# Attention, gated MLP and top-1 mixture of experts on one core: wider weight conversions, paired reciprocals, gate dots over eight steps, an earlier gather, and unscaled q with a mask per head

## The chip, the cores and the metric

One of the eight cores of a Trainium2 chip runs the whole program in one launch. The metric is device microseconds per execution. Three executions of the kernel before took 839.56, 837.05 and 837.06 us; the median is 837.06 us, and lower is better.

## What is computed

```python
# attention: 4 batches, 8 heads, 576 positions, 64 per head
scores = q @ k.T / 8 - slope[h] * abs(rel), where 0 <= rel < 128, else -1e9   # slope[h] = 2 ** -(h + 1)
x = softmax(scores) @ v                        # 2304 tokens, 512 wide
# gated MLP, 512 -> 1536 -> 512
x = ((x @ w_a) * (x @ w_b)) @ w_out
# top-1 mixture of 8 experts
logits = x @ w_gate + modality_bias[modality_id]
out = prob_of_best * (relu(x @ w1[best]) @ w2[best])
```

Inputs and output are float32. `w_a`, `w_b` and `w_out` come as float64 and are cut to float32 on the chip by integer operations on their two 32-bit words.

## The kernel before, in words

**Work.** The 2304 tokens are 18 tiles of 128, in seven chunks `c` of 3, 2, 2, 3, 3, 3 and 2 tiles. For a chunk, attention is done one (head pair `hp`, tile `t`) item at a time, 12 items for chunk 0, and then the MLP runs over 12 steps `j` of 128 hidden columns: 24 matmuls for the two products (L512), a product of the two on VectorE, and the output matmuls (L525 in chunk 0, L529 after it), which are issued one step late. While chunk `c` is in its MLP, the items of chunk `c+1` are woven in. The last part gathers tokens by expert: a first big tile of 384 tokens, then five more (`big(u)`, u = 0 to 4), a small one of 64 tokens that starts inside u = 2, and what is left under conditions.

**Float32 products.** Most matmuls run in the type float32r, with each operand split into a high and a low part and three products taken. A split is a copy on ScalarE (the high part) and a subtraction on VectorE (the low part).

**Order.** All of attention of chunk 0 is ordered by hand (`manual_schedule`, L756 to L850): every engine takes its instructions in program order there. Each turn `g` of the loop at L802 holds, for several items at once, the transposes of item g (`pt_tr`), the products with v of item g-1 (`pv_mm`), the transposed output of item g-2 (`pv_tr`), the scores of item g+3 (`score_mm`), then on VectorE `score_sel` and `score_max` (L255, L261), `score_inv` (L275, L276: add 1e-9, reciprocal), and on ScalarE the copy of the transposed weights (`pt_cp`, L303; the two triangles are then cut out on GpSimd, L311 and L313), two exponentials (`score_exp`, L271) and the scaling of the output by the reciprocals (`pv_ev`, L341 on VectorE for the first head of the pair and L344 on ScalarE for the second). `conv_step` puts one or two weight conversion operations into a turn, from g = CVS = 1 on. Outside the parts ordered by hand a planner orders each engine's instructions by priority (program order, with some lines raised) and by when it takes them to be ready.

**q of chunk 0.** The scores of a head pair are taken with one array `qq` that has each head's 64 rows of q and zeros in the other 64, so that one load of k serves both. `a_load` loads q into `raw` (L156), k (L157) and v (L158); `a_prep_q` writes q, times a scale that holds 1/8 and the inverse of the head's slope, into `qq`: seven ScalarE operations (L207) and one VectorE operation (L204). With that scale one mask serves all heads: `score_max` adds `base` or `first` and multiplies by minus the slope. `make_masks` (L95 to L113) builds the masks on GpSimd and VectorE, and `qq_zero` (L184) clears the other halves on GpSimd.

**Conversions.** For each step `j` the two weights are six VectorE operations on 128x512 words (L429, L433, L437, three for each weight) and for each weight a copy on ScalarE (L444) and a subtraction on VectorE (L445). The float32 results sit in the tag `x2`, of three buffers. `slot0` (L975) does step `j+2`'s in step `j` of chunk 0, and three more operations for `w_out`.

**Gate.** For a tile of chunk 0 to 5, the eight logits are eight products with a row of `w_gate` broadcast over the partitions and summed on VectorE (`rd_dot`, L596). `rd_fetch` loads two rows (512 KB, tag `wo`, four buffers shared with `w_out`'s); steps 0 to 3 of the next chunk each fetch two rows and take both products for all tiles, then `rd_fin` does the routing.

**Gather.** `big(u)` reads the expert's number and the offset into registers of SyncE, loads the indices (L915, SyncE's queue), gathers the rows (L918, three indirect DMAs on GpSimd's queue), and loads W1 and W2 (L895, L906, SyncE's queue). At u = 2 the small tile's index, rows and weights are queued behind these. The gathered rows are transposed on TensorE (L934) while the tile before is still in its second product.

## Time and profile before

| | |
|---|---|
| three runs | 839.56, 837.05, 837.06 us; median 837.06 |
| the profiled execution's own time | 840.08 us |
| its span, first to last instruction | 838.4 us |
| granted TensorE clock, mean over the span | 0.994 |
| busy in the span: TensorE, VectorE, ScalarE, GpSimd | 812.3, 557.2, 429.8, 182.1 us |
| bytes moved | 145.37 MB, 173 GB/s in the mean |

All durations below are from the profiled execution. Times in a window or a timeline are microseconds from the span's start. Matmuls are pipelined and their ends are modelled, so a busy TensorE can still be one that is held up; what holds it is read from the waits and the chain. PE is TensorE, DVE VectorE, ACT ScalarE, POOL GpSimd, SPq SyncE's DMA queue; L12 is line 12.

### The profile page before, as it was taken

The numbers are of one execution on the slowest core, as the hardware profiler recorded it, in microseconds if no ns is written. First come the engines' busy times: TensorE is split into PE (matmuls) and PEld (weight loads), VectorE is DVE, ScalarE is ACT, GpSimd is POOL, SyncE is SP. The second block draws the span as 40 slices with busy tenths as digits, with TensorE's granted clock in tenths as the row PEclk, the third lists the DMA queues.
The fourth block names the chain that finished last, engine by engine and source line by source line (L and its number), as shares of the span: only waits on it lengthen the run. The fifth ranks groups of instructions, "written<-read, shape, count | busy, mean of one in ns | idle before, by whom it ended". The sixth has DMA issues, their size and how long they took to land.

```text
span 838.4 us, 14297 instructions
## 1 busy us (share of the span) xinstructions
PE 812.3 (97%) x4770; PEld 730.6 (87%) x4770; DVE 557.2 (66%) x1699; ACT 429.8 (51%) x1144; POOL 182.1 (22%) x245
## 2 busy tenths in 40 slices
PE   8899999999999989999999999999999999999994
PEld 6788877989989979999999999999988998979893
DVE  7799996987976875568865693377376444447320
ACT  6754465647666735665556632232336444537420
POOL 5322012113222222212222111100133030115101
PEclk9999999999999999999999999999999999999998
DMA  9995445786674774444642253647328553538301
GB/s 260 339 401 188 137 140 169 206 284 200 190 213 149 186 211 131 117 120 139 180 130 89 76 186 105 200 163 223 134 82 303 193 185 123 185 117 294 123 27 40
DMA packets 67874, 145.37 MB, mean 173 GB/s; under 512 B 12047, under 2 KB 32175, under 8 KB 67792
## 3 DMA queue, kind: packets, MB, share of 16 engines
q1 hardware_dynamic: 64240, 134.64, 51.6%
q0 software_dynamic: 3552, 9.73, 3.2%
q8 instruction: 40, 0.66, 0.3%
q14 instruction: 42, 0.34, 0.1%
HBM read 122.35 MB, written 22.12 MB: 172 GB/s over the span
## 4 chain that ended last, share of the span: by engine, by line
PE 75%; issue 8%; DMA 5%; DVE 5%; ACT 3%; POOL 2%; SPq 1%; POOLq 0%; ACTq 0%; DVEq 0%
PE ps_ab L512 32%; PE acc L529 13%; PE ps_h L1129 8%; PE ps_y L1112 7%; PE ps_o L369 4%; PE acc L525 4%; PE ps_s L247 2%; DMA wgt<-in_wgt 2%; PE ps_p L297 1%; PE ps_o L334 1%; PE ps_t L934 1%; PE ps_s L243 1%; DVE junk L596 1%; ACT p L271 1%; POOL out L1119 1%
## 5 line engine op out<-in xcount | busy, mean ns | idle before, releaser
L512 PE MATMUL ps_ab<-xr,wab 128*128 128x384 f32 (+1 forms) x2016 | 345.1, 318 | 4.7 <-DVE gf L1071 3.2
L512 PEld LDWEIGHTS ps_ab<-xr,wab 128*128 128x128 f32 x2016 | 308.5, 188 | 16.9 <-DVE gf L1071 4.7
L529 PE MATMUL acc<-wo,g 128*128 128x512 f32 x540 | 143.9, 398 | 0.0
L311 POOL TENSOR_SCALAR_AFFINE_SELECT pt<-pc 128x512 fp32r<-128x512 f32 (+1 forms) x72 | 50.4, 700 | 330.1 <-DVE pc L309 189.6
L529 PEld LDWEIGHTS acc<-wo,g 128*128 128x128 f32 x540 | 96.5, 188 | 15.3
L1129 PE MATMUL ps_h<-xT,w1s 128*128 128x384 f32 x576 | 104.2, 337 | 0.0
L1112 PE MATMUL ps_y<-w2s,h 128*128 128x512 f32 x432 | 104.1, 394 | 0.0
L1129 PEld LDWEIGHTS ps_h<-xT,w1s 128*128 128x128 f32 x576 | 99.7, 188 | 1.4 <-issue 0.5
L596 DVE CUSTOM_DVE_ANT_0 junk<-x,wgt 128x512 f32<-128x512 f32 x128 | 91.8, 717 | 12.2 <-DMA wgt<-in_wgt 8.0
L1112 PEld LDWEIGHTS ps_y<-w2s,h 128*128 128x128 f32 x432 | 79.8, 188 | 15.8
L271 ACT ACTIVATE p<-p,mx 128x128 f32<-128x128 f32 x144 | 56.8, 396 | 31.3 <-DVE mx L261 30.7
L1074 ACT CAST g<-gf 128x256 fp32r<-128x256 f32 (+1 forms) x72 | 33.0, 458 | 58.2 <-DVE gf L1071 57.9
L1071 DVE TENSOR_TENSOR gf<-ps_ab,asb 128x256 f32<-128x256 f32 (+1 forms) x72 | 35.1, 487 | 38.1 <-PE ps_ab L512 34.3
L1067 ACT COPY asb<-ps_ab 128x256 f32<-128x256 f32 (+1 forms) x72 | 30.6, 424 | 58.2 <-PE ps_ab L512 57.4
L885 DVE TENSOR_TENSOR w2s<-wr,w2s 128x1024 fp32r<-128x1024 f32 x24 | 29.4, 1225 | 38.4 <-ACT w2s L884 38.1
L313 POOL TENSOR_SCALAR_AFFINE_SELECT pt<-pc 128x512 fp32r<-128x512 f32 (+1 forms) x72 | 54.7, 760 | 0.0
L885 DVE TENSOR_TENSOR w1s<-wr,w1s 128x1024 fp32r<-128x1024 f32 x28 | 34.3, 1224 | 23.9 <-ACT w1s L884 23.9
L284 ACT ACTIVATE p<-p,mx 128x128 f32<-128x128 f32 x104 | 36.0, 394 | 25.3 <-DVE mx L276 23.8
L369 PE MATMUL ps_o<-pt,vv 128*128 128x256 f32 x312 | 48.8, 290 | 0.0
L1119 POOL DMA_INDIRECT out<-y,idx x18 | 21.4, 1187 | 116.0 <-ACT y L1118 114.5
L255 DVE COPY_PREDICATED ps_s<-upper,ps_s 128x256 f32<-128x256 uint8 x72 | 30.5, 424 | 23.8 <-PE ps_s L247 16.5
L1132 ACT ACTIVATE h<-ps_h 128x384 fp32r<-128x384 f32 x48 | 23.4, 489 | 43.7 <-PE ps_h L1129 43.7
(218 smaller groups left out, 1136.0 us busy)
## 6 DMA issues: line engine op xcount, KB each, us to landing
wo<-wo_d SPq DMA_DIRECT2D x60, 512.0 KB, 3.8
wr<-in_moe_w SPq DMA_DIRECT2D x56, 512.0 KB, 4.3
wgt<-in_wgt SPq DMA_DIRECT2D x24, 512.0 KB, 4.3
wraw<-in_moe_w_a SPq DMA_DIRECT2D x12, 512.0 KB, 8.4
wraw<-in_moe_w_b SPq DMA_DIRECT2D x12, 512.0 KB, 9.1
wor<-in_moe_w_out SPq DMA_DIRECT2D x12, 512.0 KB, 4.4
kr<-in_k SPq DMA_DIRECT2D x24, 256.0 KB, 4.2
wo_d<-wo SPq DMA_DIRECT2D x12, 512.0 KB, 3.3
```

The lines of the kernel that those rows point to most:

```text
L271: nc.scalar.activation(out=it.p[:, h, :], in_=it.p[:, h, :], func=AF.Exp, bias=it.mx[:, 2 + h:3 + h], scale=-1.0, accum_out=it.mx[:, 4 + h ...
L284: nc.scalar.activation(out=it.p[:, h, :], in_=it.p[:, h, :], func=AF.Copy, scale=it.mx[:, 6 + h:7 + h])
L311: nc.gpsimd.affine_select(out=it.pt[:, :, 0], in_=pc, pattern=pat + [[-1, P]], base=0, channel_multiplier=1, compare_op=ALU.is_gt, fill=0.0)
L313: nc.gpsimd.affine_select(out=it.pt[:, :, 1], in_=pc, pattern=pat + [[1, P]], base=0, channel_multiplier=-1, compare_op=ALU.is_ge, fill=0.0)
L369: nc.tensor.matmul(it.po, lhsT=a.vv[:, t + b, r].rearrange("p h d -> p (h d)"), rhs=it.pt[:, :, b, s, :], start=(i == 0), stop=(i == 5))
L512: nc.tensor.matmul(ps[:, :n], lhsT=w[:, m, r, kk * P:(kk + 1) * P], rhs=xr[:, s, kk, :n], start=(idx == 0), stop=(idx == len(terms) - 1))
L529: nc.tensor.matmul(acc[c, t], lhsT=g[:, r, t * P:(t + 1) * P], rhs=w[:, s, :], start=(j == 0 and idx == 0), stop=(j == NJ - 1 and idx == 2))
L596: nc.vector.tensor_tensor_reduce(out=junk, in0=x2[:, 0:DM], in1=wgt[:, k], scale=1.0, scalar=0.0, op0=ALU.mult, op1=ALU.add, accum_out=lgr ...
L885: nc.vector.tensor_tensor(out=dst[:, 1], in0=srcw, in1=dst[:, 0], op=ALU.subtract)
L1071: nc.vector.tensor_tensor(out=gf[:, :n], in0=psb[:, :n], in1=asb[:, :n], op=ALU.mult)
L1112: nc.tensor.matmul(pss[t], lhsT=h[:, r, f, t * P:(t + 1) * P], rhs=W2[f // 2][:, s_, f % 2, :], start=(f == 0 and i == 0), stop=(f == 7 an ...
L1129: nc.tensor.matmul(ps, lhsT=W1[f // 2][:, r, kk, (f % 2) * P:(f % 2 + 1) * P], rhs=xT[:, s_, kk, :], start=(kk == 0 and i == 0), stop=(kk ...
```

## The change

1. **Paired conversions.** `wab_jobs` does both weights of a step in one operation of 1024 words each: three VectorE operations, one ScalarE copy and one subtraction, in place of six, two and two. The float32 result has a tag of its own, `ff`, with one buffer. In chunk 0's attention they begin at g = 3 in place of 1, always one at a time, and stop when four are left.
2. **Paired reciprocals.** In chunks 0 and 1 two items share a tile for their sums, and the addition and the reciprocal are done once for both, at the second.
3. **Dots over eight steps.** Each of steps 0 to 7 takes one row's products; the load of two rows is in every other step.
4. **Gather ahead.** `big(u)` emits the index load and the gathers of `u+1` after its tenth group of matmuls, where it was at the start of `big(u+1)`.
5. **q unscaled.** Chunk 0's q is loaded straight into the two halves of `qq`, by two DMAs of 64 partitions in place of one of 128; `a_prep_q` does nothing there. Each head has its own pair of masks, `fb` (first and base) times 2^(2-h): two made on VectorE, six on GpSimd, ahead of the clearing of the later pairs' halves. The scale in `score_max` is -1/8 there.
6. In `pv_ev`, the first head's scaling goes to ScalarE for chunk 0's first six items. The SBUF set aside for GpSimd's DMA descriptors is 8192 bytes of a partition.

```diff
-    CVS = 1
+    CVS = 3
@@ make_masks
+        for h in range(H):
+            if h % 4 == 0:
+                mh = m1.tile([P, 4, 2, P], BF16, tag="x2", bufs=3, name="m_h")
+            masks[h] = mh[:, h % 4]
+            (nc.vector if h < 2 else nc.gpsimd).tensor_scalar(out=masks[h], in0=fb, scalar1=2.0 ** (2 - h), scalar2=None,
+                                                              op0=ALU.mult)
@@ a_load, c == 0
-            nc.sync.dma_start(out=a.qr, in_=q[rows, 0:q1])
+            for h in range(2):
+                o = 64 * h
+                nc.sync.dma_start(out=a.qq[o:o + 64, h, 0:q1], in_=q[hp * P + o:hp * P + o + 64, 0:q1])
@@ a_prep_q
+        if a.c == 0:
+            return
@@ score_max
+            if a.c == 0:
+                m, sc = masks[2 * a.hp + h][:, min(it.t, 1)], -0.125
@@ score_inv
+        if it.a.c in V32:
+            if it.half:
+                m = it.mxp
+                nc.vector.tensor_scalar(out=m[:, :, 4:6], in0=m[:, :, 4:6], scalar1=1e-9, scalar2=None, op0=ALU.add)
+                nc.vector.reciprocal(out=m[:, :, 6:8], in_=m[:, :, 4:6])
+            return
@@ pv_ev
-            if it.a.c == 0 and h == 0:
+            if it.a.c == 0 and h == 0 and it.a.hp >= 2:
@@ wab_jobs
+        def one():
+            f = m1.tile([P, 2, KD * P], U32, tag="ff", bufs=1, name="f64f")
...
+        def sp():
+            f = st[0].bitcast(F32)
+            w = wab[j] = wab_p.tile([P, 2, 2, KD * P], F32R, tag=f"wab{j}", name=f"wab{j}")
+            nc.scalar.copy(out=w[:, :, 0], in_=f)
+            nc.vector.tensor_tensor(out=w[:, :, 1], in0=f, in1=w[:, :, 0], op=ALU.subtract)
+
+        return [("d", one), ("d", lambda: more(1, 0xC0000000, ALU.bitwise_and)),
+                ("d", lambda: more(0, 29, ALU.logical_shift_right)), ("s", sp)]
@@ rd_dot
-        for k in range(2):
-            for i, t, x2, lgr in rd:
...
+        for i, t, x2, lgr in rd:
+            junk = m1.tile([P, DM], F32, tag="x2T", bufs=1, name="junk")
+            nc.vector.tensor_tensor_reduce(out=junk, in0=x2[:, 0:DM], in1=wgt[:, e % 2], scale=1.0, scalar=0.0,
+                                           op0=ALU.mult, op1=ALU.add, accum_out=lgr[:, e:e + 1])
@@ conv_step
-            if g >= CVS and len(conv) > 8:
-                kd = conv[0][0]
-                for _ in range(2 if kd == "s" else 1):
-                    if conv and conv[0][0] == kd:
-                        conv.pop(0)[1]()
+            if g >= CVS and len(conv) > 4:
+                conv.pop(0)[1]()
@@ main loop
-            if rd and R0 <= j < R0 + E // 2:
-                wgt = rd_fetch(2 * (j - R0))
+            if rd and R0 <= j < R0 + E and (j - R0) % 2 == 0:
+                wgt = rd_fetch(j - R0)
@@ big
-        pool = side()
-        idx, xg = u_gather(ld(uv, NBIG + u, E * RG - UT), 3, pool)
+        if u not in pre:
+            pre_gather(u)
+        pool, idx, xg = pre.pop(u)
...
+            if ahead and n_ == S_P:
+                pre_gather(u + 1)
@@ kernel
-    nc = bacc.Bacc("TRN2", target_bir_lowering=False, num_devices=1)
+    nc = bacc.Bacc("TRN2", target_bir_lowering=False, num_devices=1, dynamic_dma_scratch_size=8192)
```

## Rows read from the trace of the kernel before

**Rows 1.** The page, part 1: busy time and share of the span, TensorE.
```profile
PE 812.3 (97%) x4770; PEld 730.6 (87%) x4770; DVE 557.2 (66%) x1699; ACT 429.8 (51%) x1144; POOL 182.1 (22%) x245
```

**Rows 2.** Waits of TensorE over the span: total us, times, longest us.
```profile
PE ps_ab L512 <- DVE gf L1071: 3.2, 3, 2.0
PE ps_t L934 <- DMA xg<-x2d,idx: 1.6, 1, 1.6
```

**Rows 3.** Windows between the first score matmuls of successive items, chunk 0.
```profile
11.01:13.10 2.09, 2.09 (x18) 1.94 (x17) 1.61 (x8) 1.52 (x9) 0.88 (x3) 1.00 1.05 375
13.10:16.33 3.23, 2.42 (x17) 1.94 (x16) 2.86 (x11) 2.17 (x8) 0.51 (x2) 1.00 1.20 217
16.33:20.18 3.85, 3.58 (x15) 2.64 (x16) 3.58 (x19) 3.42 (x13) 2.65 (x7) 0.80 0.89 289
20.18:23.15 2.97, 2.97 (x16) 2.50 (x16) 1.44 (x9) 1.17 (x6) 1.55 (x4) 0.68 1.02 388
...
28.52:31.57 3.05, 2.25 (x18) 1.97 (x17) 2.19 (x7) 2.01 (x8) 0.51 (x2) 1.00 1.00 318
31.57:34.53 2.96, 2.53 (x16) 1.91 (x16) 2.93 (x15) 2.90 (x11) 2.15 (x6) 1.00 1.01 401
sum 26.42, PE 23.50 PEld 18.33 DVE 21.02 ACT 19.90 POOL 10.71; mean PE 2.61 PEld 2.04 DVE 2.34 ACT 2.21 POOL 1.19
```

**Rows 4.** Groups by line and shape, window 0 to 43.3.
```profile
L207 ACT ACTIVATE kk<-raw,qscale 64x384 f32<-64x384 f32 x7 | 4.3, 612 | 1.1 <-DMA raw<-in_q 1.0
L344 ACT ACTIVATE u<-ps_o,mx 128x64 f32<-128x64 f32 x12 | 3.7, 310 | 6.0 <-DVE u L341 5.9
```

**Rows 5.** Timeline, first 18 us: start, duration, instruction, [idle before].
```profile
1.26 0.42 SPq L157 DMA_DIRECT2D kk<-in_k  x1
4.03 2.91 PEld L243 LDWEIGHTS ps_s<-kk 128*128 128x128 f32 x12 [0.59 <-POOL kk L184]
7.08 0.11 POOL L724 MEMSET osum<- 128x8 bf16 x1
9.12 0.41 POOL L311 TENSOR_SCALAR_AFFINE_SELECT pt<-pc 128x256 f32<-128x256 f32 x1 [1.93 <-ACT pc L303]
17.28 0.67 DVE L437 SCALAR_TENSOR_TENSOR f64f<-wraw,f64f 128x512 uint32<-128x512 uint32 x1
17.37 0.84 POOL L311 TENSOR_SCALAR_AFFINE_SELECT pt<-pc 128x256 f32<-128x256 f32 x1 [3.77 <-ACT pc L303]
```

**Rows 6.** The page, part 6: DMA issues, KB each, us to landing.
```profile
wo<-wo_d SPq DMA_DIRECT2D x60, 512.0 KB, 3.8
kr<-in_k SPq DMA_DIRECT2D x24, 256.0 KB, 4.2
```

**Rows 7.** Groups by line and shape, window 50 to 130.
```profile
L433 DVE SCALAR_TENSOR_TENSOR f64f<-wraw,f64f 128x512 uint32<-128x512 uint32 x19 | 12.8, 689 | 0.0
L444 ACT CAST wab<-f64f 128x512 fp32r<-128x512 f32 x20 | 11.4, 617 | 5.9 <-DVE f64f L437 5.8
```

**Rows 8.** Lines L445 and L525: duration ns min/median/max, first and last start us.
```profile
L445 DVE TENSOR_TENSOR wab<-f64f,wab x24: 665/682/884, 29.5 to 128.0; 128x512 fp32r<-128x512 f32 x24
L525 PE MATMUL acc<-f64f,gf x72: 591/592/648, 51.8 to 144.9; 128*128 128x512 f32 x72
```

**Rows 9.** Windows of chunks 1 to 3: PE, PEld, DVE, ACT, POOL busy, clock, DMA.
```profile
150.00:180.00 30.00, 28.66 (x204) 26.21 (x203) 29.65 (x83) 17.77 (x51) 4.82 (x6) 1.00 0.78 240
...
212.00:245.00 33.00, 31.64 (x236) 29.68 (x235) 32.32 (x117) 22.45 (x75) 10.58 (x12) 1.00 0.72 219
...
280.00:306.00 26.00, 23.21 (x139) 21.43 (x138) 18.07 (x62) 14.24 (x44) 4.63 (x7) 1.00 0.87 216
```

**Rows 10.** Timeline of VectorE, chunk 3: start, duration, instruction, [idle before].
```profile
301.70 0.69 DVE L596 CUSTOM_DVE_ANT_0 junk<-x,wgt 128x512 f32<-128x512 f32 x1 [5.96 <-DMA wgt<-in_wgt]
```

**Rows 11.** Timeline of SyncE's queue in tile u = 2.
```profile
719.55 10.86 SPq L906 DMA_DIRECT2D wr<-in_moe_w  x4
730.99 0.39 SPq L915 DMA_DIRECT2D idx<-tab  x1
```

More of the change, by code (lines that the diff above doesn't have):

```diff
@@ L95, in make_masks @@
     def make_masks(between):
-        for key in ("base", "first", "strad", "after"):
+        fb = const.tile([P, 2, P], BF16, name="m_fb")
+        masks["first"], masks["base"] = fb[:, 0], fb[:, 1]
+        for key in ("strad", "after"):
             masks[key] = const.tile([P, P], BF16, name=f"m_{key}")
@@ L147, in a_load @@
         if c == 0:
-            r = wab_p.tile([P, 2 * nq + 1, 2, D], F32, tag=f"wab{NJ - 2 * NP + hp}", name=f"raw0_{hp}")
-            a.qr = r[:, 0:nq].rearrange("p t h d -> p (t h d)")
-            a.vr = r[:, nq:]
+            a.vr = wab_p.tile([P, nq + 1, 2, D], F32, tag=f"wab{NJ - 2 * NP + hp}", name=f"raw0_{hp}")
             kq = wab_p.tile([P, 4 * P + 2 * MT * P], F32, tag=f"wab{NJ - NP + hp}", name=f"kk0_{hp}")
@@ L195, in a_prep_q @@
         n = a.nt * P
+        if a.c == 0:
+            return
         if a.c in S32:
-            if a.c > 0:
-                a.qq = at.tile([P, 2, MT * P], F32, tag="qq", bufs=2, name="qq")
+            a.qq = at.tile([P, 2, MT * P], F32, tag="qq", bufs=2, name="qq")
             for h in range(2):
                 o, d = 64 * h, 64 * (1 - h)
-                if a.c > 0:
-                    nc.gpsimd.memset(a.qq[d:d + 64, h, :n], 0.0)
-                if a.c == 0 and a.hp < QD and h == 1:
-                    nc.vector.tensor_scalar(out=a.qq[o:o + 64, h, :n], in0=a.qr[o:o + 64, :n],
-                                            scalar1=qscale[o:o + 64, a.hp:a.hp + 1], scalar2=None, op0=ALU.mult)
-                    continue
+                nc.gpsimd.memset(a.qq[d:d + 64, h, :n], 0.0)
                 nc.scalar.activation(out=a.qq[o:o + 64, h, :n], in_=a.qr[o:o + 64, :n], func=AF.Copy,
@@ L253, in score_sel @@
         it.p = at.tile([P, 2, P], F32, tag="p", bufs=3, name="p")
-        it.mx = at.tile([P, 8], F32, tag="mx", bufs=4, name="mx")
+        if a.c in V32 and cur_mx:
+            it.mxp, it.half = cur_mx.pop(), 1
+        else:
+            it.mxp, it.half = at.tile([P, 2, 8], F32, tag="mx", bufs=3, name="mx"), 0
+            if a.c in V32:
+                cur_mx.append(it.mxp)
+        it.mx = it.mxp[:, it.half]
         nc.vector.copy_predicated(out=it.ps[:, :, P:2 * P], mask=upper.unsqueeze(1).to_broadcast([P, 2, P]), data=it.ps[:, :, 0:P])
@@ L426, in one @@
         def one():
-            f = m1.tile([P, 4 * P], U32, name="f64f", **(dict(tag="wo", bufs=WOB) if key == "o" else dict(tag="x2", bufs=X2B)))
+            f = m1.tile([P, 4 * P], U32, tag="wo", bufs=WOB, name="f64f")
             st.append(f)
@@ L441, in f64_ops @@
         return [("d", one), ("d", two), ("d", three)]
-    def f64_split(f, w, lo_eng):
-        nc.scalar.copy(out=w[:, 0], in_=f)
-        lo_eng.tensor_tensor(out=w[:, 1], in0=f, in1=w[:, 0], op=ALU.subtract)
     def wab_load(j):
@@ L1086, in attn_moe_moe2 @@
             a_preps(g + 1)
-            if rd and R0 <= j < R0 + E // 2:
-                rd_dot(wgt, 2 * (j - R0))
-                if j == R0 + E // 2 - 1:
+            if rd and R0 <= j < R0 + E:
+                rd_dot(wgt, j - R0)
+                if j == R0 + E - 1:
                     rd_fin()
@@ L1284, in u_small, with pre_gather, big @@
             in_=y[0:HT], in_offset=None, bounds_check=N - 1, oob_is_err=False))
-    S_A, S_B, S_C = 20, 27, 4
-    def big(u, after=None, cont=None):
+    S_A, S_B, S_C, S_P = 20, 27, 4, 10
+    pre = {}
+    def pre_gather(u):
+        pool = side()
+        pre[u] = (pool,) + u_gather(ld(uv, NBIG + u, E * RG - UT), 3, pool)
+    def big(u, after=None, cont=None, ahead=False):
         ev = ld(uv, u, E - 1)
-        pool = side()
-        idx, xg = u_gather(ld(uv, NBIG + u, E * RG - UT), 3, pool)
+        if u not in pre:
+            pre_gather(u)
+        pool, idx, xg = pre.pop(u)
         W1, W2 = u_w1(ev, wrq), u_w2(ev, wrq)
```

29 lines of the change are left out of this document (14 added, 15 removed).

## The prediction

> **What bounds the kernel now.** I read the page first. TensorE is busy for 97% of the span [rows 1], so a part of the change pays only where TensorE is held up, however much work it takes off VectorE. The waits of TensorE come next: its largest are 3.2 us for VectorE's product of the two halves of the MLP and 1.6 us for gathered rows [rows 2]. That list is short because a matmul that is held up often shows as a long one, so I cut the early part into windows from the first score matmul of one item of chunk 0 to that of the next. Nine such spaces take 26.42 us; the shortest, with nothing in the way, takes 2.09 us and TensorE is busy all through it [rows 3]. The reader is to see that the long spaces hold much ScalarE work (2.17 us in 3.23, 3.42 in 3.85), and that after the space in which TensorE worked 2.42 of 3.23 us the granted clock is 0.80 and then 0.68 of full speed. So chunk 0's attention is not bound by TensorE's rate but by what it waits for. Chunk 0's MLP is: its twelve groups of output matmuls follow each other every (144.9 - 51.8 - 2.1) / 11 = 8.3 us, and VectorE's last conversion is ready at 128.0 [rows 8]. In chunks 1 to 3 TensorE stands for 1.3, 1.4 and 2.8 us in three windows [rows 9].
>
> **Term 1, chunk 0's attention.** The seven scalings of q on ScalarE are 4.3 us of an engine [rows 4], and each pair of them stands in its queue ahead of the exponentials that TensorE's next transposes need. They go. For a space without them I take 2.2 us: 2.09 is shown, and in the first six items ScalarE takes over a scaling of 0.31 us [rows 4]. Nine spaces are 19.8 us. To that come: two turns with a VectorE operation of 1024 words in place of one of 512, each longer by at most the 0.69 us of a second 512-word one [rows 7], 0.6 taken, 1.2 us; the turn with the split, which has the same ScalarE and VectorE work as today's space of 3.05 us [rows 3], 0.85; and chunk 1's own scalings, which stay in the space of 2.96 us [rows 3], 0.76. Sum 22.6 us against 26.42, a gain of 3.8. The masks for heads 2 to 7 cost GpSimd six operations that the trace doesn't show; the nearest row of 128x256 takes 0.41 us [rows 5], so 2.5 us. They stand ahead of six memsets and the constants, which end at 7.2 us; the first triangle cut starts at 9.12 us after 1.93 us of waiting [rows 5]. GpSimd would be free at 9.7, which holds that cut 0.5 us behind its place today. Term 1 is then -3.3 us. Bounds: -7.6 if all nine spaces go to 2.09 (the clock's loss is inside the 26.42); +1.0 if the masks take 0.84 us each, the longest cut in these rows, and free GpSimd only at 12.2.
>
> The split of q's load adds four DMA issues to SyncE's queue, each about 0.42 us there [rows 5]. So the first k starts 0.4 us later and the last pair's k 1.6 us later. The first scores start at 4.03 us [rows 5], but VectorE reaches them later than that, behind its masks and memsets, so I put this at nothing; if that cover is gone it is 0.4 us, which the bound above holds. A row speaks against such halves: loads of k to 64 partitions, 256 KB, land after 4.2 us, loads of twice the size to all partitions after 3.8 [rows 6]. [...]
>
> **Term 2, paired conversions and reciprocals in chunk 0's MLP.** In a step, eight conversion operations on VectorE become four of twice the width and save four starts; I take 0.3 us of VectorE. TensorE has its weights some 6 us early at the end (step 11's products start about 8.3 + 2.1 us before the last output matmul at 144.9, so near 134.5, the conversion is done at 128.7 [rows 8]), so this is worth 0. Between -0.5 (steps 1 and 2, where the lead is small) and the rival below. The single `ff` buffer adds a wait: the next step's first operation stands behind this step's subtraction, and that behind ScalarE's copy of 1024 words, at most 2 x 0.617 = 1.23 us [rows 7]. Behind it on VectorE would queue the next product of the MLP, and TensorE's output matmuls after it. The cover is the three operations of `w_out` and the items of chunk 1; as forecast they fill it. The reciprocals save about 0.15 us an item on VectorE and pass no wait on, since they are wanted only after the products with v.
>
> **Term 3, dots over eight steps.** The same products, no fewer, move apart: three or two a step in place of six or four. Today VectorE waits 5.96 us at one load of gate rows [rows 10], with TensorE's product work behind it: the 2.8 us that TensorE stands in that window [rows 9]. With one load in two steps, a buffer of `wo` comes free a step before it is wanted. I take the 2.8 us and a quarter of the 2.7 us of the other two windows, where VectorE is busy 29.65 of 30 and 32.32 of 33 us [rows 9]: -3.5 us. Bounds: -5.5 (all three); +0 if the planner's new order sets a stall of the same size elsewhere. What moves along: four loads a chunk, now at steps 0, 2, 4 and 6, on SyncE's queue; `rd_fin`, now behind step 7, with its writes of rows and table. In chunk 6, whose rows are gathered at the end, four steps still follow.
>
> **Term 4, gather ahead.** TensorE waits 1.6 us for gathered rows once [rows 2]. Those gathers wait for an index load that SyncE issues at 730.99, right behind the last four loads of the small tile's weights, which took from 719.55 to 730.41 to find buffers [rows 11]. In the changed program the index load of u + 1 still comes after these in program order. So I take 0; bounds -2.5 (that wait and the gap around it) and 0. The smaller descriptor memory I put at 0 as well.
>
> **Sum:** -3.3 + 0 - 3.5 + 0 = -6.8 us. The profiled execution took 840.08 us, 3.0 above the median of the runs shown; from it the changed kernel's would take 833.3, and from the median, which I predict, 837.06 - 6.8 = 830.3.
>
> **The rivals.**
> *A, the attention stage gains nothing.* GpSimd's masks run late, and the first cut with them, or k lands late: term 1 is 0 and the time 833.6. For it: GpSimd has no slack left by my sum, and one cut took 0.84 us beside a VectorE operation with two inputs [rows 5]. Against: only the first items depend on it. [...] Chance 0.17.
> *B, the dots' stall only moves.* The planner orders chunks 1 to 6 anew and another wait appears: term 3 is 0, 833.6. For it: VectorE stays full in those windows. Against: the stall has a plain cause, a late load. Chance 0.14.
> *C, slower: VectorE becomes the bound of chunk 0's MLP.* Its place is the wait between the third conversion operation and the subtraction, once a step. If w us of it stay unfilled in each of 11 steps, TensorE loses 11w less the lead of 6 and the 3.3 us saved; it turns the forecast round from w = 1.5. At w = 1.8, the copy of 1.23 and 0.6 behind an exponential, the loss is 10.5 and the time 830.3 + 10.5 = 840.8. For it: one buffer, and ScalarE's copies had waited for VectorE 5.8 us there already [rows 7]. Against: there is other work to fill it. Chance 0.10.
> *D, the gather does come earlier,* as the change says: term 4 is -2.5, 827.8. For it: the planner may put the load first if it takes buffers to be late. Chance 0.13.
> *E, both terms fail* by A and B at once: 837. Chance 0.06.
>
> **How the numbers follow.** The forecast has 0.40; with the rivals that is 1. Range: the forecast's own is about 827 to 834 (terms 1 and 3 each off by half of themselves); 825.0 to 836.0 takes in A, B and D and leaves out C, part of E and a double success, some 0.18. Repeats of this kernel cannot tell 0.3%, 2.5 us, from no change, so faster means below 834.5: the forecast, D, and A and B in most of their spread, 0.76. Same: E and the edges of A and B, 0.15. Slower, above 839.6: C in most of its spread, 0.09.
>
> **What would show it.** In the changed profile the first score matmuls of items 4 to 12 should follow each other at about 2.2 us with two or three longer spaces, and item 12's come near 31 in place of 34.53; no clock below full between 16 and 23 us; GpSimd's first triangle cut near 9.7. Chunk 0's output matmuls should still come every 8.3 us. TensorE's wait for the product of the halves should fall from 3.2 to under 1 us, and VectorE wait under 1 us for gate rows. The index load of u = 3 should still follow the small tile's weights. The prediction is wrong if chunk 0's steps grow past 8.7 us (C), or if the spaces keep their ScalarE-free length of 2.2 only after item 6 and item 12 is not early (A).

## The result, and the profile after

The changed kernel is slower: 849.5 us in the median of four runs (847.46 to 850.57), against 838.31 us for four runs of the kernel before beside it; ratio 1.0127, 95% interval 1.0095 to 1.0159. The prediction was 830.3 us, with 825.0 to 836.0 as its range. The profiled execution took 850.57 us, its span 848.4 us, 10.0 more than before.

The start of TensorE's work in the trace shows where the time went, as after minus before, in us (items and steps are counted from 0, so item 12 is the first of chunk 1): item 4 of chunk 0's attention +3.5, item 7 +0.5, item 12 +3.5, output matmuls of step 3 of chunk 0's MLP +3.3, first output matmul of chunk 1 +5.2, of chunk 4 +11.5, first big tile of the experts +10.5, last matmul +10.3. So there are two places, chunk 0's attention and chunks 1 to 4; from the experts on the two kernels run alike.

*Chunk 0's attention.* Windows between the first score matmuls of items 3 to 12 of the changed kernel (length, busy time of TensorE, weight loads, VectorE, ScalarE, GpSimd, clock, DMA share, GB/s), to be held against [rows 3]:

```profile
9.96:14.48 4.52, 2.76 (x16) 1.87 (x15) 2.88 (x17) 1.88 (x9) 3.85 (x16) 1.00 0.96 303
14.48:16.58 2.10, 2.10 (x18) 1.95 (x17) 0.94 (x2) 2.10 (x10) 0.70 (x3) 1.00 1.08 246
16.58:18.62 2.04, 2.04 (x18) 1.89 (x17) 1.85 (x13) 1.75 (x11) 0.92 (x3) 1.00 0.66 163
18.62:20.66 2.04, 2.04 (x18) 1.89 (x16) 1.99 (x12) 1.82 (x10) 0.51 (x2) 1.00 0.63 23
20.66:26.34 5.68, 2.46 (x18) 1.99 (x16) 3.68 (x12) 1.86 (x10) 4.28 (x10) 1.00 0.98 333
26.34:30.04 3.70, 3.70 (x18) 3.24 (x16) 1.04 (x6) 1.85 (x10) 0.91 (x3) 0.54 1.11 341
...
sum 28.09, PE 21.93 PEld 18.60 DVE 19.03 ACT 17.76 POOL 15.00; mean PE 2.44 PEld 2.07 DVE 2.11 ACT 1.97 POOL 1.67
```

Where nothing holds it, a space is 2.04 to 2.10 us: without the scalings of q the loop does run at that pace. Three spaces (4.52, 5.68, 3.70) undo it. The last of them has no idle TensorE, only a granted clock of 0.54, after 3.2 us of standing in the one before. What stood is in GpSimd's timeline of the changed kernel (start, duration, instruction, idle before):

```profile
3.65 5.15 POOL L115 TENSOR_SCALAR m_h<-m_fb 128x256 bf16<-128x256 bf16 x6 [0.74 <-DVE m_fb L108]
8.86 2.71 POOL L193 MEMSET kk<- 64x384 f32 x6
12.93 0.41 POOL L334 TENSOR_SCALAR_AFFINE_SELECT pt<-pc 128x256 f32<-128x256 f32 x1
21.42 0.50 POOL L772 CAST mid<-mid_i 128x18 f32<-128x18 int32 x1 [2.29 <-DMA mid_i<-in_moe_modality_id]
23.36 1.35 POOL L782 TENSOR_TENSOR bm<-bm,tb 128x144 f32<-128x144 f32 x1
24.67 0.40 POOL L334 TENSOR_SCALAR_AFFINE_SELECT pt<-pc 128x256 f32<-128x256 f32 x1
```

GpSimd first waits 0.74 us for the mask `fb` that VectorE makes; the six masks then take 0.86 us each (5.15 / 6), and the first cut comes at 12.93 us in place of 9.12 [rows 5]. Later the cut at 24.67 us stands behind the bias constants, which wait 2.29 us for their load.

*SyncE's queue* of the changed kernel, timeline and waits:

```profile
8.48 1.39 SPq L165 DMA_DIRECT2D kk<-in_q  x2
11.31 1.45 SPq L165 DMA_DIRECT2D kk<-in_q  x2
14.35 0.33 SPq L166 DMA_DIRECT2D kk<-in_k  x1
16.71 0.49 SPq L736 DMA_DIRECT2D wg<-in_moe_w_gate  x1
17.94 0.37 SPq L740 DMA_DIRECT2D mid_i<-in_moe_modality_id  x1
42.30 0.68 SPq L469 DMA_DIRECT2D wraw<-in_moe_w_a  x1
```

```profile
SPq L167 <- DMA wraw<-in_moe_w_b: 1.6, 1, 1.6
SPq L166 <- DMA wraw<-in_moe_w_a: 1.6, 1, 1.6
```

The last k of chunk 0 waits for a weight load that was issued eight DMAs before it. Before the change, the load that waited for the same weights (0.9 us) was the gate's, again the eighth behind it; it went out at 11.38 us, here at 16.71. Wait and timeline of the kernel before:

```profile
SPq L706 <- DMA wraw<-in_moe_w_a: 0.9, 1, 0.9
```

```profile
11.38 0.38 SPq L706 DMA_DIRECT2D wg<-in_moe_w_gate  x1
```

In the records of both kernels SyncE's loads signal eight semaphores in turn, all through the span, and none goes out before the eighth ahead of it has landed: none of the 347 loads behind the first eight before the change, none of the 351 after it, with 39 and 42 of them within 0.1 us of that landing and sizes from 0.2 to 768 KB. So in these programs a further load moves those that follow: the first weight load behind the table's eight DMAs goes out at 42.30 us, before at 37.41. What the DMA engines moved in the first 40 us, first of the changed kernel, then of the kernel before, 1.14 MB more:

```profile
DMA packets 10248, 10.66 MB, mean 266 GB/s; under 512 B 3607, under 2 KB 8971, under 8 KB 10244
```

```profile
DMA packets 11005, 11.80 MB, mean 295 GB/s; under 512 B 3759, under 2 KB 9647, under 8 KB 11001
```

*TensorE's waits* over the span, and the dots' group:

```profile
PE ps_o L357 <- POOL pt L334: 4.9, 2, 3.2
PE ps_ab L543 <- DVE gf L1098: 2.7, 4, 1.3
PE ps_s L254 <- DVE pc L332: 2.5, 1, 2.5
PE ps_s L250 <- ACT qq L212: 2.4, 2, 1.6
PE ps_o L392 <- POOL pt L334: 2.4, 1, 2.4
PE ps_t L961 <- DMA xg<-x2d,idx: 1.7, 1, 1.7
```

```profile
DVE junk L626 <- DMA wgt<-in_wgt: 31.4, 14, 6.2
```

The waits of [rows 2] are still there: 2.7 us for the product of the halves (was 3.2) and 1.7 for the gathered rows (was 1.6). Others have come beside them: for cuts in chunk 0 (4.9) and at the start of chunk 4 (2.4), for a subtraction on VectorE in chunk 3 (2.5), and for chunk 1's q, which lands late (ScalarE waits 5.8 us for it between 44 and 70 us; before it waited for none there). VectorE waits 31.4 us for gate rows, where it waited 8.0 before.

### The profile page after: what moved, and what is told of

Read it like the earlier page. It is cut to its first block, busy times and chain, and to the rows that moved or that the text cites. A ratio compares the mean times of both kernels' runs of the same rounds, so it can differ in the third digit from the quotient of the medians.

```text
span 848.4 us, 14197 instructions
## 1 busy us (share of the span) xinstructions
PE 814.0 (96%) x4770; PEld 735.0 (87%) x4770; DVE 549.6 (65%) x1626; ACT 422.7 (50%) x1131; POOL 188.3 (22%) x251
## 4 chain that ended last, share of the span: by engine, by line
PE 60%; DVE 11%; DMA 11%; issue 10%; ACT 3%; POOL 2%; SPq 1%; POOLq 0%; ACTq 0%; DVEq 0%
PE ps_ab L543 26%; PE acc L560 12%; PE ps_h L1156 7%; PE ps_y L1139 6%; PE ps_o L392 4%; DMA wgt<-in_wgt 3%; PE ps_s L254 2%; DMA wraw<-in_moe_w_b 2%; DVE junk L626 1%; PE acc L556 1%; DVE f64f L485 1%; DMA qr<-in_q 1%; PE ps_p L320 1%; DMA x2d<-zrow 1%; DMA idx<-tab 1%
## 5 line engine op out<-in xcount | busy, mean ns | idle before, releaser
L334 POOL TENSOR_SCALAR_AFFINE_SELECT pt<-pc 128x512 fp32r<-128x512 f32 (+1 forms) x72 | 53.4, 741 | 339.2 <-DVE pc L332 192.8
L626 DVE CUSTOM_DVE_ANT_0 junk<-x,wgt 128x512 f32<-128x512 f32 x128 | 91.3, 713 | 38.2 <-DMA wgt<-in_wgt 31.4
L336 POOL TENSOR_SCALAR_AFFINE_SELECT pt<-pc 128x512 fp32r<-128x512 f32 (+1 forms) x72 | 54.2, 753 | 0.0
L392 PEld LDWEIGHTS ps_o<-pt,vv 128*128 128x128 f32 x312 | 43.1, 190 | 5.4 <-POOL pt L334 2.6
```

The costliest lines, as they stand in the source:

```text
L334: nc.gpsimd.affine_select(out=it.pt[:, :, 0], in_=pc, pattern=pat + [[-1, P]], base=0, channel_multiplier=1, compare_op=ALU.is_gt, fill=0.0)
L336: nc.gpsimd.affine_select(out=it.pt[:, :, 1], in_=pc, pattern=pat + [[1, P]], base=0, channel_multiplier=-1, compare_op=ALU.is_ge, fill=0.0)
L392: nc.tensor.matmul(it.po, lhsT=a.vv[:, t + b, r].rearrange("p h d -> p (h d)"), rhs=it.pt[:, :, b, s, :], start=(i == 0), stop=(i == 5))
L626: nc.vector.tensor_tensor_reduce(out=junk, in0=x2[:, 0:DM], in1=wgt[:, e % 2], scale=1.0, scalar=0.0, op0=ALU.mult, op1=ALU.add, accum_out ...
```

## The experiments

Each ratio is against runs of the kernel before beside it on the same chip. The right-hand columns are the shift of TensorE's work against the trace of before, in us; "end" is the last matmul. The runs e4, e8, e10 to e12, e14, e15 and e18 hold the smaller descriptor memory too, and e12 and e15 the gather ahead.

| run | median us | ratio, 95% interval | item 12 | chunk 0 step 3 | chunk 1 | chunk 4 | end |
|---|---|---|---|---|---|---|---|
| after | 849.5 | 1.0127 (1.0095-1.0159) | +3.5 | +3.3 | +5.2 | +11.5 | +10.3 |
| e1 dots back | 842.83 | 1.0066 (1.0045-1.0086) | +2.6 | +2.8 | +4.1 | +5.4 | +2.3 |
| e2 dots alone | 849.65 | 1.0140 (1.0114-1.0166) | +0.8 | +0.8 | +0.9 | +10.9 | +9.7 |
| e3 q back | 846.91 | 1.0106 (1.0083-1.0129) | +3.1 | +2.5 | +3.8 | +9.0 | +7.5 |
| e4 q alone | 847.41 | 1.0133 (1.0108-1.0159) | +2.9 | +5.1 | +7.0 | +5.4 | +4.7 |
| e5 constants late | 842.59 | 1.0043 (1.0026-1.0060) | +2.9 | +3.0 | +4.2 | +4.8 | +0.3 |
| e6 masks on VectorE | 841.0 | 1.0037 (1.0019-1.0055) | +4.5 | +2.3 | +2.5 | +2.0 | +1.1 |
| e7 three at once | 841.25 | 1.0038 (1.0017-1.0059) | +0.6 | -0.6 | -0.3 | 0.0 | -0.2 |
| e8 small parts | 837.01 | 0.9975 (0.9962-0.9988) | -2.1 | -0.3 | -0.3 | -2.4 | -2.5 |
| e18 reciprocals | 838.87 | 1.0004 (0.9982-1.0025) | -1.7 | +1.8 | +1.8 | +1.8 | +2.0 |
| e9 split alone | 843.95 | 1.0064 (1.0044-1.0084) | +3.2 | +4.8 | +6.1 | +4.9 | +4.2 |
| e13 split by columns | 841.14 | 1.0027 (1.0008-1.0046) | +0.7 | +0.7 | +0.7 | +0.1 | -0.2 |
| e12 table late | 837.99 | 0.9995 (0.9980-1.0011) | -1.8 | -0.8 | -0.8 | -2.4 | -3.2 |
| e10 conversions alone | 840.56 | 1.0034 (1.0022-1.0046) | +0.6 | +1.1 | +2.1 | +3.3 | +0.5 |
| e16 q and dots back | 840.59 | 1.0031 (1.0014-1.0049) | +0.4 | +1.5 | +2.3 | +2.9 | -0.1 |
| e11 dots, rows ahead | 845.06 | 1.0088 (1.0057-1.0119) | +0.1 | 0.0 | +1.3 | +4.2 | +5.2 |
| e14 chunk 4 in four | 844.53 | 1.0059 (1.0039-1.0080) | -0.8 | +0.7 | +2.1 | +5.7 | +6.0 |
| e15 rows ahead only | 844.82 | 1.0073 (1.0052-1.0094) | +0.6 | +0.6 | +1.9 | +7.9 | +7.9 |
| e17 one v later | 850.99 | 1.0125 (1.0089-1.0162) | +1.2 | +1.3 | +1.4 | +10.4 | +12.7 |

How far a shift can be read: e8 and e18 turned out to hold the same instructions in the same order on all five engines, and their traces differ by 2.1 us at chunk 0's step 3 and 4.5 at the end. A profile is one execution; a shift below some 2 us in one trace says little, and the ratios carry the verdicts. The ratios of these two, 0.9975 and 1.0004, lie 0.29% apart as well, and their intervals barely overlap: so a ratio of 0.3 to 0.4% (e5 to e7, e10, e13, e16) is near the least that these runs can tell.

### Which part costs

e1 puts the dots back into four steps (`rd_fetch(2 * (j - R0))` in steps 0 to 3, two rows' products each); e2 has the change's dots in the kernel before; e3 puts back q's single load, scaling and shared masks; e4 has the unscaled q and its masks alone.

> The changed kernel with the gate's dots put back to four steps, two rows a step; all else of the change stays. Two theories share the changed kernel's loss of some 10 us by its own marks: chunk 0's attention is 3.5 us late at item 12, the rest comes in chunks 1 to 4. Theory D (dots): the rest is the later gate rows, which VectorE waits for 31.4 us in place of 8.0. Then this kernel takes about 849.5 - 6.8 = 842.7 us, and VectorE's wait for gate rows is back near 8 us. Theory Q (attention, and the new order behind it): the dots cost nothing of themselves; then 848 to 850 us.

> The kernel before with the dots over eight steps alone. Theory D: 838.3 + 6 = about 844 us, with the loss between the first output matmuls of chunk 1 and of chunk 4. Theory Q: 837 to 840 us. My prediction's term 3 would be 834.8 us.

> The changed kernel with chunk 0's q loaded in one DMA, scaled on ScalarE and VectorE, and the old masks; paired conversions and reciprocals, dots over eight steps and the gather ahead stay. Theory Q: item 12's first scores come back to 34.5 us or earlier, and the time to 849.5 - 3.5 = 846 us or below. Theory D: what is left against the kernel before is the dots' 6 us, so 844 to 846 us; if the dots cost nothing, 838 to 840 us.

> The kernel before with unscaled q and a mask for each head alone (the masks in a tag of their own, the descriptor memory 8192 bytes). Theory Q: first triangle cut near 12.9 us in place of 9.12, item 12 at 37 to 38 us in place of 34.5, time 838.3 + 3.5 = about 842 us. My prediction's term 1 would be 835 us. Theory D leaves it at 837 to 840 us.

Both theories are right that their part costs. Undoing the dots gives back 6.7 us (849.5 - 842.83), as theory D expected to 0.1; by the ratios, each against its own runs of the kernel before, it is 0.61%, 5.1 us. e2 and e4 came out above every range given for them: the dots alone cost 1.40%, 11.7 us, and unscaled q alone 1.33%, 11 us, where theory D gave 6 and theory Q 3.5. So the parts do not add: both with all else cost 1.27%. e3 came out above its ranges too (846.91 against 846 or less), and its item 12 is still 3.1 us late although q is as before, so the paired conversions cost something in the attention. With e16 (below) the ratios make a ladder that does add: 0.31% with q and dots as before, 0.66% with the change's q added (e1), 1.27% with the dots as well. As far as ratios from different chips can be set side by side, the dots are the largest part of the changed kernel's loss, some 5 us, and q and the rest make some 3 us each.

### Chunk 0's attention: GpSimd's queue

```diff
e5 and e7, on e1:
-    CJ = 3
+    CJ = 11
e6 and e7, on e1:
-            (nc.vector if h < 2 else nc.gpsimd).tensor_scalar(out=masks[h], ...
+            nc.vector.tensor_scalar(out=masks[h], ...
e7: the DMA of k stands ahead of the two of q
```

> The changed kernel with the dots put back to four steps (842.83 us when it ran) and the bias constants of GpSimd moved from the turn g = 3 to the last turn of chunk 0's attention, g = 11. Theory P (GpSimd's queue): the cuts of items 7 and 8 wait behind those constants, which VectorE's 1024-word conversions hold up; then the spaces from item 7 to 9 fall from some 5.7 and 3.7 us to about 2.2 to 3, item 12 comes 3 to 5 us earlier and the time is 838 to 840 us. Rival: VectorE's wider conversions hold the cuts themselves (one cut took 1.40 us beside one), and the constants' place does not matter: 842 to 843 us.

> The changed kernel with the dots put back and all eight pairs of masks made on VectorE in place of six on GpSimd. Theory P: the first triangle cut comes near 9.1 to 9.6 us in place of 12.9, and item 4's scores near 11 in place of 15; the time falls by 2 to 3.5 us to 839.5 to 841. Rival: VectorE, longer by 6 x 0.28 = 1.7 us at the start, holds the first selection up by as much: 842 to 844 us.

> The changed kernel with the dots put back, the masks on VectorE, the bias constants at g = 11 and k loaded ahead of the two halves of q. If theory P tells all of the attention's loss, then the mechanism of my term 1 is left: item 12's first scores near 30 to 31 us (34.53 before), and 842.8 - 6 = about 835 to 837 us. If the wider conversions cost of themselves, 839 to 842 us.

At its places theory P holds. In e5 the spaces from item 7 to 9 fall to 2.38 and 2.04 us:

```profile
20.65:23.03 2.38, 2.26 (x17) 1.97 (x16) 2.38 (x10) 1.86 (x10) 1.91 (x4) 1.00 0.98 251
23.03:25.07 2.04, 2.04 (x17) 1.89 (x16) 2.01 (x6) 1.37 (x7) 0.36 (x1) 1.00 1.02 388
```

But its time did not follow: 842.59, the rival's range, where theory P gave 838 to 840. In e6 the first cut comes at 9.85 us and item 4 only 0.6 us late; eight masks on VectorE take 1.91 us together, 0.24 each. The bias constants are still at their old place there, and from GpSimd's timeline of e6 it is they that make item 8 and item 12 late: they wait for their load, the cut stands behind them, and TensorE waits 4.59 us for that cut.

```profile
21.30 0.63 POOL L773 CAST mid<-mid_i 128x18 f32<-128x18 int32 x1 [5.05 <-DMA mid_i<-in_moe_modality_id]
24.82 0.41 POOL L334 TENSOR_SCALAR_AFFINE_SELECT pt<-pc 128x256 f32<-128x256 f32 x1
```

In e7 item 11 is 2.6 us early. But item 12 is not, and the time stayed at 841.25 where 835 to 837 was expected: that expectation missed. The timelines of VectorE and TensorE in e7 show what was late next:

```profile
34.07 0.64 DVE L452 TENSOR_SCALAR f64f<-wor 128x512 uint32<-128x512 uint32 x1 [2.63 <-DMA wor<-in_moe_w_out]
```

```profile
35.16 2.04 PE L250 MATMUL ps_s<-kk,qq 128*128 128x256 f32 x4 [2.73 <-DVE xr L385]
```

A conversion of `w_out`, which nobody needs yet, waits 2.63 us for its load until 34.07 us; the subtraction `xr` stands behind it on VectorE and starts at 34.63, and behind that stands chunk 1's first item. The same stands in e5: the conversion waits 3.69 us there and TensorE 2.58. An attention that is early meets loads that are not. The ratio of e7, 1.0038, is that of the conversions without any change to q (e10 and e16 below, 1.0034 and 1.0031): with masks, constants and k moved, these runs leave nothing to put down to q, though the split is still in it.

### The small parts

> The kernel before with the paired reciprocals, the gather ahead and the smaller descriptor memory alone: the parts that I put at nothing. Expected 836.5 to 839 us, within 0.3% of before. If the planner's new order alone costs something, it shows here: above 840 us.

> The kernel before with the paired reciprocals and the smaller descriptor memory, without the gather ahead. If the paired reciprocals made the 1.7 us that these parts gained with the gather ahead (the trace of that kernel has 2.4 us of its gain before the gathered part begins, 0.1 to 0.4 us in it): 836 to 837.5 us. If the gather ahead made it: 838 to 839 us.

e8 came out at 0.9975, within the expected range. e18 leaves the gather ahead out, and its instructions stand in the same order on every engine as e8's: emitting the index load earlier in the program moves nothing, since the planner orders it into the same place. So e8 and e18 are two measurements of one order, 0.9975 and 1.0004: the paired reciprocals with the smaller descriptor memory are worth nothing that these runs can tell (e18's 838.87 us fell into the range that stood for the gather ahead, which cannot have made it), and no version here is shown to beat the kernel before.

### The loads

```diff
e9, on before:
-            nc.sync.dma_start(out=a.qr, in_=q[rows, 0:q1])
+            for h in range(2):
+                o = 64 * h
+                nc.sync.dma_start(out=a.qr[o:o + 64], in_=q[hp * P + o:hp * P + o + 64, 0:q1])
e13, on before:
+            for h in range(2):
+                m = slice(h * q1 // 2, (h + 1) * q1 // 2)
+                nc.sync.dma_start(out=a.qr[:, m], in_=q[rows, m])
e12, on e8: the eight table DMAs of consts_ad moved to step 4 of chunk 0's MLP
```

> The kernel before with nothing changed but chunk 0's q loaded by two DMAs of 64 partitions in place of one of 128 (into the same place, scaled as before). Theory L (loads): chunk 0's MLP cannot begin its steps 1 to 3 before its weights have landed, since the DMA engines are full from 44 to 70 us, and the half loads put SyncE's queue back: in the changed kernel the load of the gate's weights goes out at 16.71 us in place of 11.38, and 10.66 MB have moved in the first 40 us in place of 11.80, which at 400 GB/s is 2.9 us. Then the output matmuls of steps 1 to 3 come 2 to 4 us later here too and the time is 840 to 842 us. Rival M (masks and constants on GpSimd make all of it): no change, 837 to 839.5 us.

> The kernel before with chunk 0's q loaded by two DMAs of half the columns and all 128 partitions, in place of one. Theory H (half the partitions): the cost of the split by partitions (843.95 us) is not there, 837 to 840 us, and each DMA, 96 KB, lands in well under the 4.8 us that the 96 KB halves took in the changed kernel. Rival I (issues): four more DMAs on SyncE's queue cost as much however they are cut: 842 to 845 us.

> The kernel before with the paired reciprocals, gather ahead and smaller descriptor memory (837.0 us when it ran) and the eight DMAs that fill the table, 1.35 MB, moved from 28 us on SyncE's queue to step 4 of chunk 0's MLP. Theory L: the weights of steps 1 to 3 land some 3 us earlier, the output matmuls of step 3 follow, and the time is 833 to 835.5 us. If the loads do not bound those steps: 836 to 838 us.

Splitting q's load by partitions, and nothing else, costs 0.64%, 5.4 us: more than theory L's 840 to 842 us, and rival M is out. As many DMAs cut by columns cost 0.27%, with an interval that only just excludes no change. The window 8 to 16 us of the kernel before, and the windows 8 to 16 and 16 to 24 us, of e9 and then of e13:

```profile
8.00:16.00 8.00, 7.18 (x44) 5.62 (x44) 6.11 (x32) 5.85 (x22) 2.31 (x6) 1.00 1.12 309
```

```profile
8.00:16.00 8.00, 6.43 (x38) 5.20 (x37) 4.39 (x26) 4.70 (x19) 1.54 (x4) 1.00 1.02 276
16.00:24.00 8.00, 6.47 (x37) 4.58 (x36) 6.42 (x28) 5.72 (x21) 3.51 (x9) 1.00 0.69 162
```

```profile
8.00:16.00 8.00, 7.80 (x50) 6.47 (x49) 6.20 (x35) 5.31 (x21) 2.31 (x6) 1.00 1.02 322
16.00:24.00 8.00, 6.05 (x34) 4.22 (x34) 6.57 (x30) 6.17 (x23) 4.73 (x12) 1.00 0.95 275
```

At the same busy share of 1.02 the DMA engines move 276 GB/s with the halves and 322 with the full-width pieces; but the kernel before moves 309 at a share of 1.12, no more for its share than e9 (276 and 271 for a share of 1), so the rates alone do not tell the halves from whole loads. Then the queue of e9 runs dry: a share of 0.69, while SyncE waits 1.8 and 1.6 us for the weights eight loads back. The gate's load goes out at 17.14 us in e9, 14.02 in e13, 11.38 before. So the runs lean to theory H for most of it and to rival I for the smaller part. That is not fully shown: e13's 841.14 us lies between the ranges of the two, its pieces also differ from the halves in the length of a row (768 bytes in place of 1536), and whether they land sooner, as H expected, its trace does not show. Why the halves cost more than the columns, no run here shows.

A late queue is not a fixed price either. In e7 the gate's load goes out at 16.62 us and the first weight load behind the table at 41.88, nearly as late as in e9 (17.14 and 42.20), and its ratio is 1.0038. What the split costs depends on who waits for the loads that it moves. In e9 that is the first conversion, at g = 1, which nobody needs yet (before, VectorE waited 0.63 us there): VectorE's timeline has

```profile
14.75 0.43 DVE L431 TENSOR_SCALAR f64f<-wraw 128x512 uint32<-128x512 uint32 x1 [2.63 <-DMA wraw<-in_moe_w_a]
```

and behind it stand VectorE's and ScalarE's scaling of the output, for which TensorE waits 1.40 us at 15.77. It waits 1.31 us more at 25.30, for a cut behind the bias constants. In e7 the conversions begin at g = 3 and the constants stand at g = 11.

e12 missed its expectation: with 1.35 MB taken out of the way step 3 is no earlier than in e8 (-0.8 and -0.3). That bytes alone bound the first MLP steps is not borne out.

### The paired conversions

e10 is the kernel before with the change's `wab_jobs`, `conv_step` and CVS = 3; e16 is the changed kernel with q and the dots as before.

> The kernel before with the paired conversions alone. My term 2 is 0: 837 to 839.5 us. Theory W (wide): an operation of 1024 words holds GpSimd's work up twice as long as one of 512, so cuts of up to 1.4 us and the constants beside them stretch, the spaces from item 7 to 9 grow by some 3 to 4 us and TensorE runs at half clock after it: 840.5 to 843 us.

> The changed kernel with q's load, masks and scaling and the dots as before: what is left is the paired conversions, the paired reciprocals, the gather ahead. From 840.56 us for the conversions alone and the 1.7 us that the small parts gained: 838 to 840 us. If the parts don't add, up to 843 us.

Theory W's range holds, at its lower edge: 840.56 and 840.59 us, +0.34 and +0.31%; e16 was expected 0.6 us lower. In e3, whose attention has these conversions and the old q, GpSimd's and VectorE's timelines show a cut beside one of them:

```profile
21.74 1.40 POOL L328 TENSOR_SCALAR_AFFINE_SELECT pt<-pc 128x256 f32<-128x256 f32 x1
```

```profile
21.62 1.24 DVE L477 SCALAR_TENSOR_TENSOR f64f<-wraw,f64f 128x1024 uint32<-128x1024 uint32 x1
```

The cut lasts until the 1024-word operation has ended and 0.28 us more, where it takes 0.41 alone and took 0.84 beside a 512-word one [rows 5]. In e10 a product of the bias constants took 1.41 us in the same way and TensorE waited 1.9 us for the cut behind it. From item 7 to item 10 the time grew by 2.6 us (item 7 at -1.8, item 10 at +0.8), and the granted clock was 1.00 in all these spaces: the half clock that theory W expected is not there. Nor is GpSimd's hold all of it. The space from item 7 to 8 is 4.39 us, before 2.97; but the one from item 9 to 10 is 4.51, before 3.06, and what stands in it is VectorE's subtraction, which waits for ScalarE's copy of 1024 words. VectorE's timeline of the kernel before, then those of VectorE and TensorE in e10:

```profile
29.51 1.29 DVE L445 TENSOR_TENSOR wab<-f64f,wab 128x512 fp32r<-128x512 f32 x2 [0.62 <-ACT wab L444]
```

```profile
27.29 1.23 DVE L472 TENSOR_TENSOR wab<-f64f,wab 128x1024 fp32r<-128x1024 f32 x1 [2.18 <-ACT wab L471]
```

```profile
29.11 0.33 PE L351 MATMUL ps_ot<-ident,u 128*128 128x128 f32 x1 [1.57 <-ACT u L344]
```

The wait was 0.62 us before and is 2.18 here, 2.5 in e16. Behind the subtraction on VectorE stands the scaling of the output, behind that ScalarE's, and TensorE waits 1.57 us. That is the wait of rival C, in the attention and not in the MLP.

### The dots

```diff
e11, on e2:
-        wgt = m1.tile([P, 2, DM], F32, tag="wo", bufs=WOB, name="wgt")
+        wgt = m1.tile([P, 2, DM], F32, tag="wgt", bufs=2, name="wgt")
...
+                wgt = rd_fetch(0) if j == R0 else nxt
+                nxt = rd_fetch(j - R0 + 2) if j - R0 + 2 < E else None
e14, on e11: for c == 4, two rows a step in steps 0 to 3
e15, on before: that tag and the rows a step ahead, dots in four steps
e17, on e2:
-            upto('o', do_pv, g - OG)
+            upto('o', do_pv, g - OG - (c == 4 and j == 0))
```

> The kernel before with the dots over eight steps (847.4 to 849.7 us so far, with VectorE waiting for gate rows 31 us) and the rows in two buffers of their own, each pair loaded a step pair ahead. Theory G (late gate rows): VectorE no longer waits for them, and the time is back at 837 to 840 us, or below by the 2.8 us that the kernel before lost there. Rival O (order): the dots stand in the way of the next chunk's preparation on VectorE in steps 4 to 7, whenever the rows land: 844 us or more.

> The kernel with dots over eight steps and rows ahead (845.06 us), chunk 4's dots put back to four steps. Theory O (order): TensorE's wait of 2.3 us for the first triangle cut of chunk 4's step 0, and the half clock after it, are gone; chunk 4's first output matmuls come about 5 us earlier, and the time is 839.5 to 841.5 us. If that stall has another cause, 844 to 846 us.

> The kernel before with its dots in four steps, the gate rows in two buffers of their own and each pair loaded a step ahead (with the gather ahead and the smaller descriptor memory). My term 3 took the 2.8 us that TensorE stands near 302 us to come from a late load: if so they go, and the time is 834.5 to 836.5 us. If the planner's order decides, anything from 836 to 844 us.

> The kernel before with the dots over eight steps (849.65 us), and in chunk 4's step 0 one item's product with v called a step later, so that it stands behind the 24 matmuls of the next products on TensorE. If the order is the price of that place, the wait of 2.3 to 2.5 us and the half clock behind it go, chunk 4's first output matmuls come 4 to 5 us earlier against the kernel before, and the time is 844.5 to 846 us. If VectorE is simply too late there, another wait of the same size takes its place: 848 to 850 us.

With rows ahead VectorE waits 5.4 us for them in place of 32.7, and the kernel gains 4.6 us (849.65 - 845.06): theory G tells that much. 7 us stay, as rival O expected (844 us or more). 5 of them lie at one place, the change from chunk 3 to chunk 4. TensorE's timeline and a window there, in e11:

```profile
379.84 0.96 PE L369 MATMUL ps_o<-pt,vv 128*128 128x256 f32 x6
383.14 0.63 PE L369 MATMUL ps_o<-pt,vv 128*128 128x256 f32 x3 [2.34 <-POOL pt L311]
383.60 3.80 PE L512 MATMUL ps_ab<-xr,wab 128*128 128x384 f32 x12
```

```profile
384.00:388.00 4.00, 4.00 (x17) 4.00 (x17) 4.00 (x11) 2.32 (x7) 1.79 (x3) 0.59 0.27 71
```

TensorE stands 2.34 us for a cut; behind it the granted clock is 0.59, and twelve matmuls take 3.80 us. The same wait stands in the changed kernel (2.4) and in e2, e3, e14 and e15 (2.3 each). In the order of the kernel before, 24 matmuls of the next products stand ahead of that item; here they stand behind it. e14 shows that the number of chunk 4's dots does not make it: the wait stays, and the 839.5 to 841.5 us of theory O were missed. e15 (844.82 us, just above its range) shows that spreading does not either: with dots in four steps, other buffers and earlier requests it is there. (e15's gather ahead and descriptor memory stand in e8 too, which does not have the stall.) But the requests of e15 brought its rows no earlier where it counts: VectorE waits 7.1 us for rows in all, and at the load of [rows 10] 5.14 in place of 5.96:

```profile
301.06 0.69 DVE L596 CUSTOM_DVE_ANT_0 junk<-x,wgt 128x512 f32<-128x512 f32 x1 [5.14 <-DMA wgt<-in_wgt]
```

e17 puts the matmuls back in front: from the start of chunk 3's last output matmuls to that of chunk 4's first it is then 11.8 us, against 14.3 in e2 and 9.2 before. But two waits of 1.25 and 0.55 us take the old one's place, and 850.99 us is above both of its ranges. So the order is shown to make half of that place's price, and the kernel's time does not follow even that.

## Why the prediction was wrong, step by step

The largest miss is term 3: -3.5 us forecast, 5 to 7 us lost in the changed kernel and 11.7 alone. Then come term 1, -3.3 forecast and some 3 us lost with q, and term 2, 0 forecast and 2.6 us lost.

*"I put this at nothing; if that cover is gone it is 0.4 us."* The split of q's load. This step failed plainly: 5.4 us alone. I looked at who waits for q, and found VectorE behind its masks. But behind q on SyncE's queue stand k, the bias index, the weights and chunk 1's q, and they go out later with it: the gate's load at 17.14 us in e9 in place of 11.38. The price that I worked out, 0.4 us, is that of one late load; the price measured is that of all who wait for the loads behind it, and in e9 those are a conversion and the bias constants, ahead of work that TensorE wants. The row of the first scores that I went by does not show the queue.

*"The nearest row of 128x256 takes 0.41 us."* A mask took 0.86, near the 0.84 of my bound. The first cut came at 12.93 us, later than the 12.2 of that bound, since GpSimd waited 0.74 us for the mask `fb` before it began; the sum had no such wait. The bound was also added up wrongly: a cut 3.1 us late against a gain of 3.8 gives -0.7, not +1.0. With the masks on VectorE the cut came at 9.85, so rival A's place was right; its price of 0 gained was too kind.

*The spaces of 2.2 us.* Right where nothing else held them: 2.04 to 2.10. The nine together are 28.09 us, forecast 22.6, before 26.42. What failed is that the sum had no step for the bias constants: they were not in the diff, but their load was queued behind q, and they sit on GpSimd ahead of a cut.

*That an earlier end of attention is a gain of the kernel.* I took term 1 one for one to the end. In e7 and e8 the lead of 2 to 2.6 us at item 11 is 0.6 or less at chunk 0's step 3. In e7 a load of `w_out` is late next; in e8 it is a cut for chunk 1, for which TensorE waits 1.00 us at 47.28, and the granted clock is 0.60 from 48 to 52 us.

*Term 2, 0.* The bound was a gain, and rival C a slower MLP. From the output matmuls of step 1 to those of step 11 the changed kernel takes 146.8 - 67.8 = 79.0 us, the kernel before 142.8 - 64.5 = 78.3, so C did not happen there. The starts saved came to more than the 0.3 us a step that I took, for which no row stood: in the window 50 to 130 us the eight operations of a step before took 2 x (0.461 + 0.689 + 0.700 + 0.691) = 5.08 us in the mean, the four of the changed kernel 0.694 + 2 x 1.236 + 1.238 = 4.40. The loss of 2.6 us (840.56 - 837.98 in e10) shows in the attention, at two places of some 1.4 us each. One is the longer hold on GpSimd, whose row (0.84 us beside a 512-word operation) I had cited under rival A and not doubled for the wider one. The other is C's own wait, for the copy of 1024 words: I had looked for it in the MLP alone, and in term 1 I gave the turn with the split today's space of 3.05 us. The mechanism was on my list, its place was not.

*Term 3, -3.5 with bounds of -5.5 and 0.* The step that failed is "with one load in two steps, a buffer of `wo` comes free a step before it is wanted". VectorE's wait for rows went from 8.0 to 31.4 us. The loads still go out only when an output matmul lets a buffer of `wo` go: SyncE waits for these 34.6 us in 8 loads of e2, up to 7.4, where it was 40.2 us in 12 loads before. And 0 was no bound: I let the planner's new order cost at most what the stall had cost, and with the late rows it cost 5.1 to 11.7. That the stall of 2.8 us has "a plain cause, a late load" is not shown either way: in e15 the row was nearly as late as before. But in e8 VectorE waits 4.4 us at that load and TensorE stands 1.15 of 26 us, in e11 3.8 and 0.76, so a wait of that size need not cost TensorE 2.8. The slips in the sum itself are small: by its terms rival B is 833.8 us, not 833.6.

*Term 4, 0.* Right, with its reason: the order of the index load did not change.

*The chances.* Slower had 0.09, all of it for rival C in the MLP. The split, the masks, the wider conversions and the dots could each cost more than they gave, and I gave the chance of a loss to one mechanism of one of them.

What stays open: why the rows come later when they are asked for in every other step, beyond the wait for buffers, and what in the planner's estimates turns the order at chunk 4. The runs show the price of that place, that half of it goes with the order, and that neither the number of the dots nor their spread is needed for it.

## What to carry to other kernels

A load that is split or moved is priced by who waits for the loads behind it on its queue, not only by who waits for the load itself (5.4 us for q's load in e9, where I had put 0.4 at most). Where a planner writes the order, undo a part and measure: its bounds do not come from the stalls that exist today. An operation made wider to save starts can hold GpSimd's work beside it up for longer (a cut of 0.41 us took 1.40 beside 1024 words), and what reads its result waits longer for it (2.18 us for 0.62): look up what stands behind either.
